# Second weight's operand six built in the first half's chunks from operand seven's sum instead of beside keys and values

## Chip, cores and metric

The kernel runs on one core of one Trainium2 chip. The metric is the device time of one execution in microseconds (us). Three timed runs of the kernel before gave a median of 1102.75 us (1098.13 to 1105.87).

## The reference, cut to what matters

x has 2048 tokens of 576 numbers; the hidden layer of the second block has 4608.

```python
xn = layernorm(x)
q, k, v = split(xn @ wqkv)                  # 32 heads of 18
pq, pk = phi(q), phi(k)                     # phi(t) = (t+1 if t > 0 else exp(t)) + 1e-6
s = (pq @ (pk^T v)) / (pq . sum(pk) + 1e-6) @ wo
h = gelu(xn @ w1 + b1)                      # 2048 x 4608
g = silu(h @ w2 + b2)                       # w2: 4608 x 576
out = x + s * g
```

All of it is in float32. The change concerns how the weight `w2` of the product `h @ w2` is prepared.

## The kernel before

**Number format.** TensorE multiplies in a rounded 32-bit format. Each operand is therefore kept as two tiles: `hi`, the rounded copy, which ScalarE (ACT) makes by a cast, and `lo`, what the rounding left, which VectorE (DVE) makes by subtracting `hi` from the source. A product is then three matmuls per pair of operands: hi times hi, hi times lo, lo times hi.

**Seven products for eight.** Both matrix products of the second block are done as 2x2 block products in a scheme of seven multiplications. For `h @ w2`, `w2` is cut into nine chunks of 512 rows (`NC = 9`, named c), and each chunk into four blocks B00, B01, B10, B11 (row half, then column half), each 128 partitions x 576. The seven right-hand operands are, by their numbers in the code:

```text
1: B00        2: B10        3: B11        7: B11 - B01        5: B01 - B00
6: B11 - (B01 - B00) = operand 7 + B00
4: B10 - operand 7 - B00 = B10 - operand 6
```

The seven left-hand operands come from the gelu results of the same chunk: 1, 2, 4 are gelu tiles themselves, 7, 5, 6, 3 are sums made by GpSimd (POOL) in `HOps.S` (lines 1243 to 1252).

**Stages.** (1) "Keys and values": a loop over 16 tiles of 128 tokens makes the layer norm, keys, values and the state pk^T v (about 0 to 145 us of the span). (2) Queries, attention and the folded output weight, 145 to 283 us. (3) The second block in two halves of 1024 tokens each, nine chunks a half; chunk c of the first half starts at about 283.2 + 44.7 c us. The first half makes the operands of w1 and w2 from the raw weights, multiplies with them and stores them in device memory; the second half loads them back. (4) The end, from about 1065 us.

**Work on w2 in stage 1.** Beside the token tiles, `w2_load` (line 392) loads three blocks of chunk c (864 KB), `w2_sum` (line 402) makes on POOL operand 5 in place of B00 and then operand 6 in place of B11, `w2_hi` (line 407, ACT) and `w2_lo` (line 415, DVE) split each into hi and lo, and `w2_store` (line 420) writes each operand (576 KB) to device memory. `W2_AT` gives the token tile at which chunk c's sums are made; hi, lo and store follow one tile later.

**A chunk of stage 3.** Time in a chunk is counted in 28 steps, each one block of TensorE (PE) work of about 1.6 us. Steps 0 to 6 and 7 to 13 are two "Up" rounds: seven products of w1 operands with x, in the order `UP`, whose PSUM results are combined by DVE and passed through gelu by ACT. Steps 14 to 27 are the seven products with w2 operands in `ORDER`, two PSUM tiles each (q2 = 0, 2); after each, DVE adds the tile into `macc` (line 1292).

```python
UP = (1, 6, 7, 5, 2, 3, 4)
ORDER = (1, 2, 7, 4, 5, 3, 6)
PW2 = {2: 0, 1: 1, 7: 3, 4: 5, 3: 8}                     # operand: step of hi; lo is one step later
for k, i in enumerate(UP):                               # round j of chunk `step`, base = 28 * step
    u.step(i)                                            # seven matmuls, then DVE / ACT on their PSUM
    h.add(j, u.g)
    at_step(base + 7 * j + k)                            # what the plans put at this step
```

The emission order fixes the order of instructions on PE, DVE, ACT and POOL (`in_order`), so a planned instruction that has to wait holds up all that follows on its engine. All DMAs are issued on the queue of SyncE (SP), also in order.

The parts of a chunk that matter here, with "Up 0" and "Up 1" for the two rounds:

- At step 0 POOL makes operand 7 (`sum7`, line 1200), at step 2 operand 4 in two subtractions (`sum4`, line 1205).
- `W2.hi` and `W2.lo` (lines that show in the profile as L812 and L815, the helpers `set_hi` and `set_lo`) make operands 2, 1, 7, 4, 3 at the steps of `PW2`. `W2.lo` also issues the store for the second half, except in chunk 8.
- Operands 5 and 6 are loaded from device memory by `W2.load` (line 1223), for the next chunk at steps 23 and 27 (`W2_SUMS_NEXT`), for chunk 0 at steps 6 and 10 (`W2_SUMS_FIRST`).
- `HOps` (plan `PH`) makes the left-hand operands: `S` on POOL, `hi` on ACT, `lo` on DVE, from step 7 on. A name like (1, 1) is operand 1 of round 1. For operand 1 and 2 of round 0 the lo parts stand at step 10, for (7, 0) at step 11, for (1, 1) at step 12, for (2, 1) at step 13. `S` of (7, 0) stands at step 7, of (5, 0) at step 8, of (6, 0) and (3, 0) at step 11; (6, 0) overwrites the tile that lo of (1, 0) reads.
- The first product (operand 1, step 14) orders its matmuls so that those with the lo part of (1, 1) come last.
- In the second half (chunks 9 to 17) operands come from device memory, and the last chunk works from raw weights.

Of the kernel before, what the change touches and what calls it, by code (L numbers as in the profile page):

```python
# [8 lines left out]
F32 = mybir.dt.float32  # L9
F32R = mybir.dt.float32r  # L10
# [5 lines left out]
P = 128  # L16
S = 2048
D = 576
HD = 288
# [25 lines left out]
def linear_attention_gated_ffn(ctx, tc, x, xT, wqkv, wo, w1, w1e, b1, w2, b2, out):  # L45
    nc = tc.nc
    SUB, MUL, ADD = ALU.subtract, ALU.mult, ALU.add
# [7 lines left out]
    dram = ctx.enter_context(tc.tile_pool(name="dram", bufs=1, space=bass.MemoryType.DRAM))  # L55
# [67 lines left out]
    w1_dram, w2_dram = {}, {}  # L123
# [11 lines left out]
    stw = ph1.enter_context(tc.tile_pool(name="stw", bufs=2, reuse_waits="tile"))  # L135
    w2p = ph1.enter_context(tc.tile_pool(name="w2p", bufs=2, reuse_waits="tile"))
# [249 lines left out]

    T_OPS = (5, 6)
    w2raw, w2op = {}, {}  # L390

    def w2_load(c):
        t = w2p.tile([P, 3, 2, HD], F32, tag="w2r", name=f"w2r{c}")
        nc.sync.dma_start(t.rearrange("p b a d -> p (b a d)"), w2[c][:, D:])
        w2raw[c] = t

    def w2_block(c, i):

        B11, B00, B01 = (w2raw[c][:, k] for k in range(3))
        return {5: (B00, B01, B00), 6: (B11, B11, B00)}[i]  # L400

    def w2_sum(j):
        c, i = j // 2, T_OPS[j % 2]
        dst, a, b = w2_block(c, i)
        nc.gpsimd.tensor_tensor(dst, a, b, op=SUB)

    def w2_hi(j):
        shape = [P, 2, 2, HD]
        if j % 4 < 2:
            w2op[j] = stw.tile(shape, F32R, tag="stw", name=f"w2o{j}")  # L410
        else:
            w2op[j] = w2p.tile(shape, F32R, tag="w2o", name=f"w2o{j}")
        nc.scalar.copy(w2op[j][:, 0], w2_block(j // 2, T_OPS[j % 2])[0])

    def w2_lo(j):
        c, i = j // 2, T_OPS[j % 2]
        t = w2op[j]
        nc.vector.tensor_tensor(t[:, 1], w2_block(c, i)[0], t[:, 0].bitcast(F32), op=SUB)

    def w2_store(j):  # L420
        c, i = j // 2, T_OPS[j % 2]
        w2_dram[c, i] = d = dram.tile([P, 2, 2, HD], F32, name=f"op_{c}_{i}")
        nc.sync.dma_start(d, w2op.pop(j).bitcast(F32))

# [30 lines left out]
    WE_SUMS = {2 * q + 1: q for q in range(WG)}  # L457
    W2_AT = (2, 4, 6, 8, 10, 11, 12, 13, 14)
    W2_LOADS = {0: 0, 1: 1, 3: 2, 5: 3, 7: 4, 9: 5, 11: 6, 12: 7, 13: 8}
    W2_SUMS = {t: (2 * c, 2 * c + 1) for c, t in enumerate(W2_AT)}  # L460

    class XSums:

# [44 lines left out]
        def sum4(self, k):  # L508
            self.tt(self.t, (self.h0, self.l0)[k][:, self.B], self.t, (SUB, ADD)[k])
# [29 lines left out]
    for t in range(NT):  # L539
# [39 lines left out]
        if t + 1 < NTR:  # L579
            if t:  # L580
                k_t, _ = phi(t1, pk, f"k{t}", values)
# [13 lines left out]
            if t == 0:  # L595
                k_t, _ = phi(t1, pk, f"k{t}")
# [591 lines left out]
    class W2:  # L1188
# [10 lines left out]
        def sum7(self):  # L1199
            nc.gpsimd.tensor_tensor(self.src[7], self.src[3], self.src[7], op=SUB)  # L1200

        def sum4(self, k):

            self.src[4] = t = self.src[2]
            nc.gpsimd.tensor_tensor(t, t, self.src[(7, 1)[k]], op=SUB)

        def plain(self, f):
            k = 2 - 2 * (f % 2)
# [16 lines left out]
    class HOps:  # L1225
# [6 lines left out]
        def add(self, pr, g):  # L1232
            for (par, b), t in g.items():
                self.A[pr, b, par] = t
                self.src[{(0, 0): 1, (0, 1): 2, (1, 1): 4, (1, 0): "-"}[b, par], pr] = t
# [236 lines left out]
    )  # L1472


    PW2 = {2: 0, 1: 1, 7: 3, 4: 5, 3: 8}
    W2_SUMS_NEXT = {5: 23, 6: 27}
    W2_SUMS_FIRST = {5: 6, 6: 10}
    W2_NEXT = {1: 15, 2: 17, 7: 19, 4: 21, 5: 23, 3: 25, 6: 27}
    PH = dict(
        S={(7, 0): 7, (5, 0): 8, (6, 0): 11, (3, 0): 11, (7, 1): 13, (5, 1): 14, (6, 1): 15, (3, 1): 15},  # L1480
# [21 lines left out]
    w2t = {}  # L1502
# [8 lines left out]
    for step in range(n_chunks):  # L1511
        half, c = divmod(step, NC)
        base = step * NS
        plain = step == n_chunks - 1
        h = HOps(c)
        if half == 0:
            plan_w1(add, w1t[2 * step + 1], base, **P1)
            add(base, w2t[step].sum7)
            for k in range(2):
                add(base + 2, w2t[step].sum4, k)  # L1520
            for i, at in PW2.items():
                add(base + at, w2t[step].hi, i)
                add(base + at + 1, w2t[step].lo, i)
            if step == 0:
                for i, at in W2_SUMS_FIRST.items():
                    add(at, w2t[0].load, i)
        change = step == NC - 1
        if not plain:
            add(base + (11 if change else 7), load_we, 2 * step + 2)
            add(base + (16 if change else 14), load_we, 2 * step + 3)  # L1530
        if half == 0 and c < NC - 1:
            add(base + 0, make, W1, w1t, 2 * step + 2)
            add(base + 4, make, W1, w1t, 2 * step + 3)
            add(base + 1, lambda n=2 * step + 2, base=base: plan_w1(add, w1t[n], base, **P0))
            make(W2, w2t, step + 1)
            add(base + 22, w2t[step + 1].load_raw)
            for i, at in W2_SUMS_NEXT.items():
                add(base + at, lambda i=i, n=step + 1: w2t[n].load(i))
        elif not plain:
            add(base + (11 if change else 7), make, W1Loaded, w1t, 2 * step + 2)  # L1540
            add(base + (11 if change else 14), load_six, 2 * step + 2)
            add(base + (16 if change else 14), make, W1Loaded, w1t, 2 * step + 3)
            if step + 2 < n_chunks:
                make(W2, w2t, step + 1)
                for i, at in W2_NEXT.items():
                    add(base + at + 10 * change, lambda i=i, n=step + 1: w2t[n].load(i))
            else:
                make(W2, w2t, step + 1)

                w = w2t[step + 1]  # L1550
                add(base + 7, w.load_raw)
                for f in range(CF):
                    add(base + 22 + f, lambda f=f, w=w: (w.plain(f), w.hi(("p", f))))
                    add(base + 24 + f, w.lo, ("p", f))
        if not plain:
            if half == 0 and c == NC - 1:
                for k, at in X_AT.items():
                    add(base + at, load_x_part, k)
                add(base + 14, lambda: x_new.update(rs=load_rests(0)))
                add(base + 25, silu_first, C11)  # L1560
                for k in range(2):
                    add(base + 26 + k, combine, C12, nc.vector, slice(2 * k, 2 * k + 2))
                    add(base + 26 + k, combine, C21, nc.gpsimd, slice(2 * k, 2 * k + 2))
            for what in ("S", "hi", "lo"):
                for (i, pr), at in PH[what].items():
                    add(base + at, getattr(h, what), i, pr)
        if half == 1 and c == 0:
            add(base, silu_first, C12)
            add(base, silu_first, C21)
            add(base, combine, C22, nc.vector, slice(0, 2))  # L1570
            add(base + 1, combine, C22, nc.vector, slice(2, 4))
            add(base + 1, silu_first, C22)
        if half == 1 and c:
            for k in range(2):
                tiles = {}
                def load(k=k, t=7 + c, tiles=tiles):
                    tiles[0] = finish_tiles(k)
                    finish_load(t, k, tiles[0])
                add(base, load)
                add(base + 4, lambda k=k, t=7 + c, tiles=tiles: finish(t, k, tiles[0]))  # L1580
        if plain:
            for m in (C12, C21, C22):
                add(base + 4, combine, m, nc.gpsimd)
            for t, at in enumerate((6, 7, 12, 13, 5, 12, 12, 12)):
                add(base + at, load_xs, t)
            for b, f, at, lo in (
                (0, 0, 7, 8), (0, 1, 8, 9), (1, 0, 10, 10), (1, 1, 10, 11), (0, 2, 11, 12),
                (0, 3, 12, 13), (1, 3, 13, 13), (1, 2, 13, 13),
            ):
                add(base + at, tail_split, b, f)  # L1590
                add(base + lo, tail_lo, b, f)
        for j in range(CF // 2):
            n = 2 * step + j
            u = Up(n, w1t.pop(n), xs)
            for k, i in enumerate(UP):
                u.step(i)
                h.add(j, u.g)
                at_step(base + 7 * j + k)
        if plain:
            break  # L1600
        held = {}
        for k, i in enumerate(ORDER):
            for q2 in (0, 2):
                product(c, i, q2, [h.ops[i, 0], h.ops[i, 1]], w2t[step].ops[i], held)
                at_step(base + 14 + 2 * k + q2 // 2)
        if half == 0 and c == NC - 1:
            xs = x_operands(*(x_new[k] for k in ("h0", "l0", "h1", "l1", "s1", "s2", "s4", "rs")))
# [50 lines left out]
```

## Time and profile before

| what | us |
|---|---|
| median of three timed runs (lowest, highest) | 1102.75 (1098.13, 1105.87) |
| span of the profiled execution, first to last instruction | 1096.2 |
| stage 1 (keys and values), about | 0 to 145 |
| stage 2 (queries, attention), about | 145 to 283 |
| first half of the second block, nine chunks of 44.7 us | 283 to 686 |
| second half, eight chunks of 44.7 us and the plain last one | 686 to 1096 |

The profiled execution has no time listed beside its span; the span is 1.9 us under the fastest timed run and 6.6 us under the median. The mean granted clock of TensorE was 0.999.

How to read the rows: a row of the timeline has start and duration in us, engine, line, operation, output<-inputs by the program's names, shape, and in brackets the idle time of the engine ahead of it with what ended it. PEld is the loading of the stationary operand into TensorE, which runs ahead of the matmuls. A row of the stretches ("windows") has the busy time and the count of each engine, then the granted clock, the share of the DMA engines that was busy, and GB/s. Consecutive instructions of one engine overlap by some 0.08 us in these rows. The names `w__4896` and `w__4937` are chunk 3's operands 4 and 3.

### The profile page before, as it was taken

The numbers are of one execution on the slowest core, as the hardware profiler recorded it, in microseconds if no ns is written. First come the engines' busy times: TensorE is split into PE (matmuls) and PEld (weight loads), VectorE is DVE, ScalarE is ACT, GpSimd is POOL, SyncE is SP. The second block draws the span as 40 slices with busy tenths as digits, with TensorE's granted clock in tenths as the row PEclk, the third lists the DMA queues.
The fourth block names the chain that finished last, engine by engine and source line by source line (L and its number), as shares of the span: only waits on it lengthen the run. The fifth ranks groups of instructions, "written<-read, shape, count | busy, mean of one in ns | idle before, by whom it ended". The sixth has DMA issues, their size and how long they took to land.

```text
span 1096.2 us, 18083 instructions
## 1 busy us (share of the span) xinstructions
PE 1088.2 (99%) x6702; PEld 1008.8 (92%) x6702; DVE 829.5 (76%) x1132; ACT 491.3 (45%) x844; POOL 471.5 (43%) x403
## 2 busy tenths in 40 slices
PE   9999999999999999999999999999999999999998
PEld 8999989999898998989989989899898998989987
DVE  7787748888798888888888888667475584764856
ACT  6555555555545455454453544524234243242442
POOL 3676434323546446464554553424234143242340
PEclk9999999999999999999999999999999999999999
DMA  7898834675959558486585769978676676767452
GB/s 248 264 274 274 309 137 149 206 248 186 333 221 350 182 220 322 160 320 224 189 332 175 284 237 400 391 248 289 215 241 219 210 231 212 238 219 224 126 184 87
DMA packets 88400, 262.54 MB, mean 239 GB/s; under 512 B 11894, under 2 KB 24182, under 8 KB 85624
## 3 DMA queue, kind: packets, MB, share of 16 engines
q1 hardware_dynamic: 88312, 261.38, 69.3%
q8 instruction: 53, 0.87, 0.3%
q14 instruction: 35, 0.29, 0.1%
HBM read 164.24 MB, written 95.17 MB: 237 GB/s over the span
## 4 chain that ended last, share of the span: by engine, by line
PE 99%; DVE 1%; ACT 0%; issue 0%; POOL 0%; DVEq 0%; POOLq 0%
PE pm L1286 35%; PE a L1147 10%; PE e L1147 10%; PE zy L1147 10%; PE pk L321 6%; PE pq L321 5%; PE ps_s L788 5%; PE b L1147 5%; PE pv L321 4%; PE pd L1402 2%; PE ps_kva L382 1%; PE ptp L770 1%; PE ps_kw L707 1%; PE warm L369 0%; DVE wkv_l L364 0%; PE ps_kvb L382 0%
## 5 line engine op out<-in xcount | busy, mean ns | idle before, releaser
L1292 DVE TENSOR_TENSOR macc<-pm,macc 128x576 f32<-128x576 f32 x218 | 163.9, 752 | 49.9 <-PE pm L1286 48.4
L812 ACT CAST h_h<-g 128x512 fp32r<-128x512 f32 x204 | 121.9, 621 | 132.7 <-PE pm L1286 131.5
L815 DVE TENSOR_TENSOR h_l<-g,h_h 128x512 fp32r<-128x512 f32 x204 | 161.8, 800 | 0.0
L1252 POOL TENSOR_TENSOR mid<-g 128x512 f32<-128x512 f32 x34 | 43.9, 1292 | 108.1 <-ACT g L1155 108.1
L1246 POOL TENSOR_TENSOR g<-g 128x512 f32<-128x512 f32 x34 | 54.9, 1616 | 49.5 <-DVE h_l L815 28.4
L1155 ACT ACTIVATE g<-b,b1c 128x512 f32<-128x512 f32 x36 | 24.8, 690 | 102.5 <-DVE b L1173 102.5
L1164 ACT COPY mid<-a 128x512 f32<-128x512 f32 x36 | 21.1, 585 | 95.3 <-PE a L1147 95.3
L858 POOL TENSOR_TENSOR w1raw<-w1raw 128x256 f32<-128x256 f32 x18 | 13.3, 737 | 116.8 <-ACT h_h L812 68.2
L1167 DVE TENSOR_TENSOR mid<-b,mid 128x512 f32<-128x512 f32 x36 | 24.8, 690 | 45.0 <-PE b L1147 41.8
L1374 POOL TENSOR_TENSOR fin1l<-fin1h,fin1l 128x288 f32<-128x288 f32 x8 | 6.5, 811 | 118.4 <-DMA fin1l<-s_dram 69.6
L1249 POOL TENSOR_TENSOR g<-g 128x512 f32<-128x512 f32 x34 | 55.2, 1623 | 2.7
L1147 PE MATMUL a<-h0r,wa 128*128 128x512 f32 x144 | 50.4, 390 | 0.0
L1147 PE MATMUL a<-xh,wa 128*128 128x512 f32 x144 | 50.4, 390 | 0.0
L815 DVE TENSOR_TENSOR h_l<-mid,h_h 128x512 fp32r<-128x512 f32 x34 | 48.8, 1436 | 1.2
L1155 ACT ACTIVATE g<-e,b1c 128x512 f32<-128x512 f32 x36 | 24.8, 690 | 51.9 <-DVE e L1180 51.9
L753 POOL TENSOR_TENSOR pbuf<-phiq,den 128x576 f32<-128x576 f32 x16 | 19.4, 1213 | 63.6 <-DVE den L752 63.6
L1243 POOL TENSOR_TENSOR g<-g 128x512 f32<-128x512 f32 x34 | 44.1, 1296 | 2.7
L1180 DVE TENSOR_TENSOR e<-e,mid 128x512 f32<-128x512 f32 x36 | 24.8, 690 | 22.3 <-PE e L1147 22.3
L1170 DVE TENSOR_TENSOR mid<-zy,mid 128x512 f32<-128x512 f32 x36 | 24.9, 691 | 19.8 <-PE zy L1147 19.8
L1173 DVE TENSOR_TENSOR b<-e,mid 128x512 f32<-128x512 f32 x36 | 25.2, 700 | 18.5 <-PE e L1147 17.4
L321 PE MATMUL pk<-wkv_h,xh 128*128 128x288 f32 (+1 forms) x160 | 38.2, 321 | 0.4 <-ACT xh L248 0.4
L321 PE MATMUL pk<-wkv_l,xh 128*128 128x288 f32 (+1 forms) x160 | 38.4, 321 | 0.0
(857 smaller groups left out, 3646.5 us busy)
## 6 DMA issues: line engine op xcount, KB each, us to landing
we<-we_dram SPq DMA_DIRECT2D x36, 448.0 KB
w2raw<-w SPq DMA_DIRECT2D x10, 1152.0 KB
op<-w2o SPq DMA_DIRECT2D x18, 576.0 KB
w1raw<-w SPq DMA_DIRECT2D x18, 512.0 KB
op_a<-wa SPq DMA_DIRECT2D x18, 512.0 KB
op_c<-wc SPq DMA_DIRECT2D x18, 512.0 KB
op_d<-wd SPq DMA_DIRECT2D x18, 512.0 KB
wc<-op_c SPq DMA_DIRECT2D x18, 512.0 KB
```

Of the source, the lines that this page charges most:

```text
L321: nc.tensor.matmul(ps[:, h, : ws.stop - ws.start], st, w[:, k, ws], start=(begin and i == 0), stop=(end and i == len(seq) - 1), skip_group ...
L788: nc.tensor.matmul(ps[:, h, :HD], st[:, k, :], w[:, k, h * HD : (h + 1) * HD], start=(i == 0), stop=(i == len(seq) - 1),)
L812: nc.scalar.copy(pair[0], src)
L815: eng.tensor_tensor(pair[1], src, pair[0].bitcast(F32), op=SUB)
L1147: nc.tensor.matmul(ps, st, mv, start=first and n == 0, stop=n == len(seq) - 1, skip_group_check=True,)
L1155: nc.scalar.activation(g, ps, AF.Gelu_apprx_tanh, bias=b1c[:, f : f + 1])
L1243: tt(src[5, pr], A(1, 0), A(1, 1), op=ADD)
L1246: tt(src[6, pr], src[5, pr], A(0, 0), op=SUB)
L1249: tt(src[3, pr], A(0, 1), src[6, pr], op=SUB)
L1252: tt(src[7, pr], A(0, 0), A(1, 0), op=SUB)
L1286: nc.tensor.matmul(ps[:, q, :HD], hs[p][st][:, cs], m[:, p, :], start=(n == 0 and i not in CHAIN), stop=(n == 5), skip_group_check=True,)
L1292: nc.vector.tensor_tensor(dst, src, dst, op=ADD)
```

## The change

Stage 1 no longer loads B11 and no longer makes operand 6: per chunk it loads two blocks (576 KB), makes one sum, one hi, one lo and one store. In the first half's chunks POOL makes operand 6 as operand 7 plus B00 (in place of B00, so after B00's own hi and lo), and operand 4 as B10 minus operand 6, both now at step 3; ACT and DVE then make hi and lo of operand 6 too, and it is stored for the second half except in chunk 8. Operand 4's hi and lo move from steps 5 and 6 to 6 and 7, operand 6's are at 7 and 8, operand 3's move from 8 and 9 to 9 and 10. The loads of operand 6 in the first half are gone. The second half's loads are as before.

```diff
-    T_OPS = (5, 6)
     def w2_load(c):
-        t = w2p.tile([P, 3, 2, HD], F32, tag="w2r", name=f"w2r{c}")
-        nc.sync.dma_start(t.rearrange("p b a d -> p (b a d)"), w2[c][:, D:])
+        t = w2p.tile([P, 2, 2, HD], F32, tag="w2r", name=f"w2r{c}")
+        nc.sync.dma_start(t.rearrange("p b a d -> p (b a d)"), w2[c][:, 2 * D :])
-    def w2_block(c, i):
-        B11, B00, B01 = (w2raw[c][:, k] for k in range(3))
-        return {5: (B00, B01, B00), 6: (B11, B11, B00)}[i]
-    def w2_sum(j):
-        c, i = j // 2, T_OPS[j % 2]
-        dst, a, b = w2_block(c, i)
-        nc.gpsimd.tensor_tensor(dst, a, b, op=SUB)
-    def w2_hi(j):
-        shape = [P, 2, 2, HD]
-        if j % 4 < 2:
-            w2op[j] = stw.tile(shape, F32R, tag="stw", name=f"w2o{j}")
-        else:
-            w2op[j] = w2p.tile(shape, F32R, tag="w2o", name=f"w2o{j}")
-        nc.scalar.copy(w2op[j][:, 0], w2_block(j // 2, T_OPS[j % 2])[0])
+    def w2_sum(c):
+        B00, B01 = (w2raw[c][:, k] for k in range(2))
+        nc.gpsimd.tensor_tensor(B00, B01, B00, op=SUB)
+    def w2_hi(c):
+        w2op[c] = w2p.tile([P, 2, 2, HD], F32R, tag="w2o", name=f"w2o{c}")
+        nc.scalar.copy(w2op[c][:, 0], w2raw[c][:, 0])
...
-    W2_SUMS = {t: (2 * c, 2 * c + 1) for c, t in enumerate(W2_AT)}
+    W2_SUMS = {t: (c,) for c, t in enumerate(W2_AT)}
...
-        def sum4(self, k):
+        def sum6(self):
+            self.src[6] = t = self.src[1]
+            nc.gpsimd.tensor_tensor(t, self.src[7], t, op=ADD)
+        def sum4(self):
             self.src[4] = t = self.src[2]
-            nc.gpsimd.tensor_tensor(t, t, self.src[(7, 1)[k]], op=SUB)
+            nc.gpsimd.tensor_tensor(t, t, self.src[6], op=SUB)
...
-    PW2 = {2: 0, 1: 1, 7: 3, 4: 5, 3: 8}
-    W2_SUMS_NEXT = {5: 23, 6: 27}
-    W2_SUMS_FIRST = {5: 6, 6: 10}
+    PW2 = {2: 0, 1: 1, 7: 3, 4: 6, 6: 7, 3: 9}
...
             add(base, w2t[step].sum7)
-            for k in range(2):
-                add(base + 2, w2t[step].sum4, k)
+            add(base + 3, w2t[step].sum6)
+            add(base + 3, w2t[step].sum4)
             for i, at in PW2.items():
                 add(base + at, w2t[step].hi, i)
                 add(base + at + 1, w2t[step].lo, i)
             if step == 0:
-                for i, at in W2_SUMS_FIRST.items():
-                    add(at, w2t[0].load, i)
+                add(6, w2t[0].load, 5)
...
             add(base + 22, w2t[step + 1].load_raw)
-            for i, at in W2_SUMS_NEXT.items():
-                add(base + at, lambda i=i, n=step + 1: w2t[n].load(i))
+            add(base + 23, w2t[step + 1].load, 5)
```

More of the change, by code (lines that the diff above doesn't have):

```diff
@@ L385, in state, with w2_lo, w2_store @@
             )
-    T_OPS = (5, 6)
     w2raw, w2op = {}, {}
     def w2_load(c):
-        t = w2p.tile([P, 3, 2, HD], F32, tag="w2r", name=f"w2r{c}")
-        nc.sync.dma_start(t.rearrange("p b a d -> p (b a d)"), w2[c][:, D:])
+        t = w2p.tile([P, 2, 2, HD], F32, tag="w2r", name=f"w2r{c}")
+        nc.sync.dma_start(t.rearrange("p b a d -> p (b a d)"), w2[c][:, 2 * D :])
         w2raw[c] = t
-    def w2_block(c, i):
-        B11, B00, B01 = (w2raw[c][:, k] for k in range(3))
-        return {5: (B00, B01, B00), 6: (B11, B11, B00)}[i]
-    def w2_sum(j):
-        c, i = j // 2, T_OPS[j % 2]
-        dst, a, b = w2_block(c, i)
-        nc.gpsimd.tensor_tensor(dst, a, b, op=SUB)
-    def w2_hi(j):
-        shape = [P, 2, 2, HD]
-        if j % 4 < 2:
-            w2op[j] = stw.tile(shape, F32R, tag="stw", name=f"w2o{j}")
-        else:
-            w2op[j] = w2p.tile(shape, F32R, tag="w2o", name=f"w2o{j}")
[L413 to L423, printed above, removed]
+    def w2_sum(c):
[4 more added lines that the diff above has]
+        nc.scalar.copy(w2op[c][:, 0], w2raw[c][:, 0])
+    def w2_lo(c):
+        t = w2op[c]
+        nc.vector.tensor_tensor(t[:, 1], w2raw[c][:, 0], t[:, 0].bitcast(F32), op=SUB)
+    def w2_store(c):
+        w2_dram[c, 5] = d = dram.tile([P, 2, 2, HD], F32, name=f"op_{c}_5")
+        nc.sync.dma_start(d, w2op.pop(c).bitcast(F32))
     we = {}
```

## The prediction

> **What bounds the kernel now.** I read the page's totals first (busy time and share of the span), then the windows by stage (busy time and count of PE, PEld, DVE, ACT and POOL, clock, DMA share, GB/s), then one chunk of the first half engine by engine.
>
> ```profile
> span 1096.2 us, 18083 instructions
> PE 1088.2 (99%) x6702; PEld 1008.8 (92%) x6702; DVE 829.5 (76%) x1132; ACT 491.3 (45%) x844; POOL 471.5 (43%) x403
> ```
>
> ```profile
> 41.02:142.41 101.39, 101.39 (x626) 98.48 (x625) 80.96 (x99) 56.51 (x111) 68.00 (x62) 1.00 0.89 280
> 417.32:462.04 44.72, 44.72 (x267) 40.81 (x267) 39.18 (x52) 21.28 (x37) 23.43 (x19) 1.00 0.67 246
> ```
>
> ```profile
> 417.32:439.58 22.26, 22.26 (x100) 18.40 (x100) 18.89 (x25) 12.39 (x22) 12.96 (x10) 1.00 0.97 363
> ```
>
> TensorE is busy in all of stage 1's steady part (101.39 of 101.39 us) and in all of chunk 3 (44.72 of 44.72). Only 8.0 us of the span are without a matmul. So work taken from another engine can give back next to nothing; work put on another engine costs nothing until TensorE has to wait for it. The engine to watch is DVE: 39.18 of 44.72 us in a chunk, 18.89 of 22.26 in its two Up rounds, where the change adds its work.
>
> **What the change takes away.** In stage 1, half of these:
>
> ```profile
> L405 POOL TENSOR_TENSOR w2r<-w2r 128x576 f32<-128x576 f32 x18 | 28.8, 1598 | 15.6 <-DVE phik L340 8.5 <-DMA w2r<-w 6.4
> ...
> L418 DVE TENSOR_TENSOR w2o<-w2r,w2o 128x576 fp32r<-128x576 f32 x18 | 19.1, 1098 | 0.2
> ...
> L413 ACT CAST w2o<-w2r 128x576 fp32r<-128x576 f32 x18 | 11.5, 672 | 2.5 <-POOL w2r L405 2.5
> ```
>
> That is 14.4 us of POOL, 9.6 of DVE, 5.8 of ACT, nine stores of 576 KB, and nine loads shorter by 288 KB. TensorE's full row covers all of it: 0 us. The bounds: no loss, and a gain of no more than the 8.0 us that TensorE is idle anywhere, most of it at the start and the end, where none of this work stands; I take 0.
>
> In the first half nine loads of operand 6 go and eight stores of the same size come. DMA engines are 97% busy in the Up rounds; the load left at the head of that stretch and the store comes at its foot, so its bytes stay as they are.
>
> ```profile
> 434.78 0.33 SPq L809 DMA_DIRECT2D op<-w__4937  x1
> ...
> 462.84 0.38 SPq L1223 DMA_DIRECT2D w__5265<-op  x1
> ```
>
> On SP's queue the new store stands just ahead of the first row and the load of the second row goes. What queues behind the later stores of operands 4 and 6 is the load of `we` for the next chunk, delayed by 1 to 2 us with over 20 us in hand: 0 us. POOL has one sum and one subtraction in place of two subtractions of the same shape, behind the same instructions: 0 us.
>
> **What it adds, on the path.** Per chunk one cast on ACT and one DVE subtraction, and operand 4's pair moves one step back. The price depends on where TensorE next waits for DVE. These are chunk 3's rows of the timeline from the end of Up 0 on: DVE, then ACT, then POOL, then TensorE.
>
> ```profile
> 429.97 0.69 DVE L1184 TENSOR_TENSOR zy<-zy,mid 128x512 f32<-128x512 f32 x1
> 430.78 0.76 DVE L815 TENSOR_TENSOR w__4896<-w2raw,w__4896 128x576 fp32r<-128x576 f32 x1
> 431.89 0.69 DVE L1167 TENSOR_TENSOR mid<-b,mid 128x512 f32<-128x512 f32 x1 [0.36 <-ACT mid L1164]
> 433.27 0.69 DVE L1170 TENSOR_TENSOR mid<-zy,mid 128x512 f32<-128x512 f32 x1 [0.69 <-PE zy L1147]
> 433.88 0.87 DVE L815 TENSOR_TENSOR w__4937<-w2raw,w__4937 128x576 fp32r<-128x576 f32 x1
> 434.86 0.70 DVE L1173 TENSOR_TENSOR b<-e,mid 128x512 f32<-128x512 f32 x1
> 435.47 1.28 DVE L815 TENSOR_TENSOR h_l<-g,h_h 128x512 fp32r<-128x512 f32 x2
> 436.83 1.63 DVE L815 TENSOR_TENSOR h_l<-mid,h_h 128x512 fp32r<-128x512 f32 x1
> 438.38 0.69 DVE L1180 TENSOR_TENSOR e<-e,mid 128x512 f32<-128x512 f32 x1
> 438.98 1.18 DVE L815 TENSOR_TENSOR h_l<-g,h_h 128x512 fp32r<-128x512 f32 x1
> ...
> 442.80 0.76 DVE L1292 TENSOR_TENSOR macc<-pm,macc 128x576 f32<-128x576 f32 x1 [0.78 <-PE pm L1286]
> ```
>
> ```profile
> 430.08 0.66 ACT L812 CAST w__4896<-w2raw 128x576 fp32r<-128x576 f32 x1
> 430.69 0.69 ACT L1155 ACTIVATE g<-zy,b1c 128x512 f32<-128x512 f32 x1
> 431.28 0.58 ACT L1164 COPY mid<-a 128x512 f32<-128x512 f32 x1
> ```
>
> ```profile
> 431.46 1.30 POOL L1252 TENSOR_TENSOR mid<-g 128x512 f32<-128x512 f32 x1 [3.23 <-ACT g L1155]
> 432.84 1.30 POOL L1243 TENSOR_TENSOR g<-g 128x512 f32<-128x512 f32 x1
> 436.32 1.58 POOL L1246 TENSOR_TENSOR g<-g 128x512 f32<-128x512 f32 x1 [2.19 <-ACT g L1155]
> 437.99 1.62 POOL L1249 TENSOR_TENSOR g<-g 128x512 f32<-128x512 f32 x1
> ```
>
> ```profile
> 436.25 1.52 PE L1147 MATMUL e<-s,wc 128*128 128x512 f32 x6
> ...
> 440.61 0.32 PEld L1286 LDWEIGHTS pm<-w__4829,h_l 128*128 128x128 f32 x2
> ```
>
> The row at 438.98 is the lo part of (1, 1); it ends at 440.16. The row at 440.61 is the first load that needs it. The slack is 0.45 us. From 434.86 to there DVE has no idle time, so whatever DVE has more to do behind 434.86 comes straight off it. The change puts operand 3's lo (now at step 10) exactly there.
>
> The POOL rows show a second price. The lo part at 436.83 takes 1.63 us where the pair ahead of it takes 0.64 each: POOL's sum of 436.32 runs until 437.90, and it ends 0.56 behind that. The lo part at 438.98 ends 0.55 behind POOL's 439.61. POOL's own sum at 437.99, caught behind DVE's end at 438.46, ends 1.15 after it. DVE rows that take one input from PSUM (0.69, 0.70) show no such thing. So: a DVE subtraction caught behind a POOL sum ends 0.55 after it (0.62 for 576 columns), a POOL sum caught behind DVE 1.15 after it.
>
> The walk, each start 0.08 before the end of the row ahead, cross-engine starts 0.03 after the end waited for:
>
> - ACT: gelu 430.69 as before; hi of 4 now behind it, 431.28 to 431.94; copy of `mid` 431.89 to 432.47; hi of 6 to 433.04.
> - DVE: lo of 4 starts at 431.97 instead of 430.78, now caught behind POOL's sum (ends 432.76): ends 433.38. POOL's next sum ends 434.53.
> - `mid<-b` 433.30 to 433.99. Lo of 6, caught behind POOL's 434.53, ends 435.15. `mid<-zy` ends 435.76, `b<-e` 436.38 (before: 435.56). TensorE's matmul of 436.25 adds into the bank that `b<-e` reads: it waits 0.15.
> - Lo of 3 ends 437.06, lo of (1, 0) 437.66, lo of (2, 0) 438.26. POOL's sum, which overwrites what (1, 0) reads, is released at 437.7, caught behind (2, 0), ends 439.41.
> - Lo of (7, 0) ends 439.97, POOL's next sum 441.12, `e<-e` 440.58, lo of (1, 1) 441.67.
> - The load at 440.61 starts at 441.70: TensorE stands 1.09 us, the 0.15 included.
>
> Later in the chunk DVE had 0.78 us idle waiting for TensorE (row 442.80), and `macc` keeps its place ahead of the chained product, so the lag ends there and does not add up from chunk to chunk. Ends far apart: if nothing collides, DVE is late by one lo (0.68 beyond overlap) less 0.45 of slack, 0.26 with the 0.03: 2.3 us in all. If each caught instruction took its full solo time behind the other (0.68 or 0.76, and 1.30), the same walk ends the lo of (1, 1) at 442.65 and TensorE stands 2.07: 18.6 us. I take 1.09, since the caught rows of this very place gave its two constants.
>
> The Trainium skill, page "SBUF — State Buffer", section "Who interferes with whom", says that a DVE instruction with two SBUF inputs contends with a GpSimd instruction that reads SBUF, and that the one issued first holds the shared pair for the whole instruction while the other fully blocks. The rows agree that one waits for the other, though the one caught ends 0.55 after, not a full 0.68, so here it had done a little beforehand. By the rule taken strictly the sum would be the 18.6 us just given.
>
> All nine chunks of the first half carry the same rows; the first and the last:
>
> ```profile
> 304.83 1.18 DVE L815 TENSOR_TENSOR h_l<-g,h_h 128x512 fp32r<-128x512 f32 x1
> ...
> 662.57 1.18 DVE L815 TENSOR_TENSOR h_l<-g,h_h 128x512 fp32r<-128x512 f32 x1
> ```
>
> ```profile
> 306.46 0.32 PEld L1286 LDWEIGHTS pm<-w__3385,h_l 128*128 128x128 f32 x2
> ...
> 664.20 0.32 PEld L1286 LDWEIGHTS pm<-w__7225,h_l 128*128 128x128 f32 x2
> ```
>
> The slack is 0.45 in both. So 9 x 1.09 = 9.8 us: a span of 1106.0. The median of the runs lies 6.55 above the span; added to it, 1112.55, say 1112.5, slower by 0.9%. One per cent (11.0 us) is about what a measurement of this kernel can tell from no change.
>
> **The rivals.**
>
> - *No collision.* DVE and POOL slide past each other, only the shift of one lo remains: +2.3 us, 1105. For it: DVE is idle 0.36 and 0.69 in this very place. Against: the POOL sums follow gelu and DVE, they slide along. Chance 0.16.
> - *Full blocking.* Caught instructions take their full time: +18.6 us, 1121; anything from 1.22 us a chunk on passes one per cent. For it: the lo part of 1.63 us. Against: 0.55, twice. Chance with all that lies between 1.22 and 2.07: 0.34.
> - *Not slower: stage 1 gives it back.* Timed runs lie 1.9 to 9.7 us above the span. If that excess is the transfers of stage 1 (89% busy), 8.0 MB less at 280 GB/s is 28 us of transfer time, which could bring a run down to the span: -6.5 us, 1096. It decides only if TensorE waits for transfers there and nothing stands in the chunks. Against: its full row. Chance 0.06, half of it by over one per cent with what I don't see.
> - *The change doesn't do what it says.* Operand 6 made late for its product (step 26)? It is there at step 8, 18 steps early; nothing speaks for it, and it gets no chance of its own.
>
> **How the numbers follow.** The forecast (0.8 to 1.2 us a chunk) has 0.44. Slower by over 1%: 0.34 of full blocking and what lies between, and 0.03 of the forecast's upper edge with the scatter of runs: 0.37. Faster by over 1%: 0.03. Within 1%: 0.60. The range reaches from 1102 (no collision, less run scatter) to 1119 (1.8 us a chunk), which leaves out the last of full blocking and the gain; the forecast's own range is 1109 to 1114.
>
> **What would show it.** Right: TensorE's loads in the first product wait for DVE once a chunk, chunks of 45.5 to 46 us in the first half and still 44.7 in the second; lo of operand 4 over 1.2 us long; stage 1 as long as before with DVE 9 us less busy. Wrong: a first-half chunk under 45.0 us (no collision), over 46.2 (full blocking), a wait at another place, or a shorter stage 1.

## The result, and the profile after

The changed kernel takes 1111.83 us (median of four runs, 1111.43 to 1112.2). The kernel before takes 1100.82 us, the median of the three runs above and one more beside the changed kernel (1098.13 to 1105.87). That is a ratio of 1.009, 95% interval 1.0061 to 1.012, 11.0 us slower. The forecast was 1112.5. The near hit of the time hides two errors. The span was forecast at 1106.0 and came out at 1110.4, 14.2 us longer than before instead of 9.8. The median was forecast 6.55 above the span and lies 1.4 above it. That 4.4 too little and 5.1 too much nearly cancel is luck, and most of what follows is about these two errors.

The page's first lines and the windows of the kernel after (busy time and count of PE, PEld, DVE, ACT, POOL, then clock, DMA share, GB/s): stage 1, chunk 3 of the first half, one chunk of the second half.

```profile
span 1110.4 us, 18032 instructions
PE 1094.7 (99%) x6702; PEld 1008.3 (91%) x6702; DVE 826.0 (74%) x1132; ACT 491.7 (44%) x844; POOL 459.8 (41%) x394
```

```profile
41.02:142.14 101.12, 101.12 (x625) 98.24 (x624) 63.61 (x90) 51.19 (x101) 52.97 (x54) 1.00 0.81 215
421.98:468.36 46.38, 45.48 (x267) 40.76 (x267) 40.77 (x53) 21.90 (x38) 23.82 (x19) 1.00 0.67 237
...
722.49:767.17 44.68, 44.68 (x268) 40.80 (x268) 28.34 (x39) 14.56 (x25) 14.86 (x13) 1.00 0.74 250
```

Stage 1 ends 0.27 us earlier and DVE is 17 us less busy in it. A chunk of the first half takes 46.37 us instead of 44.72, 1.65 more; nine of them are 14.9. A chunk of the second half is as before. Now PE is not busy all of the chunk (45.48 of 46.38). The 0.90 us of idle time are only part of the 1.65: the matmuls behind a wait take longer too (the six behind the first wait 1.67 us for 1.52). What its weight loads waited for (engine, tile, line, what it waited for: us in total, times, longest):

```profile
PEld pm L1276 <- DVE h_l L802: 6.2, 9, 0.7
PEld e L1134 <- DVE b L1160: 5.6, 9, 0.6
PEld pm L1276 <- ACT h_h L799: 4.3, 9, 0.5
```

Three waits, each once in each of the nine chunks. The kernel before had none of them. Chunk 3 again, DVE first; these rows stand 4.66 us later than those of before, as chunk 3 itself does (421.98 for 417.32). `w__4859`, `w__4876` and `w__4904` are operands 4, 6 and 3.

```profile
436.63 1.39 DVE L802 TENSOR_TENSOR w__4859<-w2raw,w__4859 128x576 fp32r<-128x576 f32 x1 [1.32 <-ACT w__4859 L799]
437.95 0.68 DVE L1154 TENSOR_TENSOR mid<-b,mid 128x512 f32<-128x512 f32 x1
438.55 1.25 DVE L802 TENSOR_TENSOR w__4876<-w2raw,w__4876 128x576 fp32r<-128x576 f32 x1
439.73 0.68 DVE L1157 TENSOR_TENSOR mid<-zy,mid 128x512 f32<-128x512 f32 x1
440.51 0.70 DVE L1160 TENSOR_TENSOR b<-e,mid 128x512 f32<-128x512 f32 x1
441.12 0.75 DVE L802 TENSOR_TENSOR w__4904<-w2raw,w__4904 128x576 fp32r<-128x576 f32 x1
441.78 1.29 DVE L802 TENSOR_TENSOR h_l<-g,h_h 128x512 fp32r<-128x512 f32 x2
442.99 1.79 DVE L802 TENSOR_TENSOR h_l<-mid,h_h 128x512 fp32r<-128x512 f32 x1
444.70 0.69 DVE L1167 TENSOR_TENSOR e<-e,mid 128x512 f32<-128x512 f32 x1
445.30 1.18 DVE L802 TENSOR_TENSOR h_l<-g,h_h 128x512 fp32r<-128x512 f32 x1
...
454.43 0.74 DVE L1282 TENSOR_TENSOR macc<-pm,macc 128x576 f32<-128x576 f32 x1
```

POOL, then the loading side of TensorE, in the same chunk:

```profile
436.12 1.29 POOL L1242 TENSOR_TENSOR mid<-g 128x512 f32<-128x512 f32 x1 [3.23 <-ACT g L1142]
437.49 1.70 POOL L1233 TENSOR_TENSOR g<-g 128x512 f32<-128x512 f32 x1
```

```profile
441.26 1.24 PEld L1134 LDWEIGHTS e<-s,wc 128*128 128x128 f32 x6 [0.62 <-DVE b L1160]
...
446.53 0.30 PEld L1276 LDWEIGHTS pm<-w__4782,h_l 128*128 128x128 f32 x2 [0.67 <-DVE h_l L802]
```

```profile
454.37 0.32 PEld L1276 LDWEIGHTS pm<-w__4815,h_h 128*128 128x128 f32 x2
...
455.30 0.30 PEld L1276 LDWEIGHTS pm<-w__4859,h_h 128*128 128x128 f32 x2 [0.47 <-ACT h_h L799]
```

The lo part of operand 4 (436.63) is caught behind POOL's sum of 436.12, takes 1.39 for 0.76, and ends 0.61 after it. POOL's next sum is caught behind that in turn and ends 1.17 after it; the lo part of operand 6 is caught behind this sum and ends 0.61 after it. `b<-e` comes at 440.51 and the load of 441.26 waits for it: first wait. Operand 3's lo follows, then the lo parts of the first product, and (1, 1) ends at 446.48: second wait. The third stands at the first load of operand 4's product, 455.30. The view names ACT's cast, but the tile that this product adds into is freed by the DVE row of 454.43, which ends at 455.17; which of the two it is was tried below.

### The profile page after: what moved, and what is told of

Same layout as the page of the kernel before. It is cut to its first block, busy times and chain, and to the rows that moved or that the text cites. A ratio compares the mean times of both kernels' runs of the same rounds, so it can differ in the third digit from the quotient of the medians.

```text
span 1110.4 us, 18032 instructions
## 1 busy us (share of the span) xinstructions
PE 1094.7 (99%) x6702; PEld 1008.3 (91%) x6702; DVE 826.0 (74%) x1132; ACT 491.7 (44%) x844; POOL 459.8 (41%) x394
## 4 chain that ended last, share of the span: by engine, by line
PE 87%; DVE 7%; issue 2%; DMA 2%; POOL 1%; ACT 1%; SPq 0%; DVEq 0%; POOLq 0%
PE pm L1276 30%; PE a L1134 8%; PE zy L1134 8%; PE e L1134 7%; PE pk L321 6%; PE pq L321 5%; PE ps_s L775 5%; PE b L1134 5%; PE pv L321 4%; DVE h_l L802 4%; PE pd L1392 2%; PE ps_kva L382 1%; PE ptp L757 1%; PE ps_kw L694 1%; DVE macc L1282 1%
## 5 line engine op out<-in xcount | busy, mean ns | idle before, releaser
L1236 POOL TENSOR_TENSOR g<-g 128x512 f32<-128x512 f32 x34 | 54.9, 1614 | 60.9 <-DVE h_l L802 59.5
L1239 POOL TENSOR_TENSOR g<-g 128x512 f32<-128x512 f32 x34 | 55.2, 1624 | 2.7
L1233 POOL TENSOR_TENSOR g<-g 128x512 f32<-128x512 f32 x34 | 47.6, 1401 | 2.7
L775 PE MATMUL ps_s<-kw_h,th 128*128 128x288 f32 x160 | 35.5, 303 | 0.0
```

The costliest lines, as they stand in the source:

```text
L775: nc.tensor.matmul(ps[:, h, :HD], st[:, k, :], w[:, k, h * HD : (h + 1) * HD], start=(i == 0), stop=(i == len(seq) - 1),)
L1233: tt(src[5, pr], A(1, 0), A(1, 1), op=ADD)
L1236: tt(src[6, pr], src[5, pr], A(0, 0), op=SUB)
L1239: tt(src[3, pr], A(0, 1), src[6, pr], op=SUB)
```

## The experiments

**Theories.** Two errors need a cause. For the chunks, A: the cost is place, not load. DVE is late where the new and moved lo parts stand ahead of something TensorE waits for, and is made later by being caught behind POOL sums; put elsewhere, the same work is free. B, the rival: the first half's chunks have no room left on DVE and ACT, so the work costs about the same wherever it stands. For the second error, C: stage 1's lighter transfers bring timed runs down to the span. D: they are worth nothing, and the spread of the runs of before (8 us here) comes from elsewhere. Each experiment has runs of the kernel before beside it. For operand 6 later, operand 4's pair back, the third wait and stage 1 alone these are the same 30 runs, median 1099.68 (1097.25 to 1107.8). For order without work, before again, transfers kept and work kept they are another 26, median 1100.88 (1098.47 to 1108.59).

**Operand 6 later, 4 and 3 where they were.** On the changed kernel:

```diff
-    PW2 = {2: 0, 1: 1, 7: 3, 4: 6, 6: 7, 3: 9}
+    PW2 = {2: 0, 1: 1, 7: 3, 4: 5, 3: 8, 6: 19}
```

> The changed kernel with operands 4 and 3 back at their old steps (hi 5 and 8, lo 6 and 9) and operand 6's hi and lo at steps 19 and 20, where no POOL sum runs and DVE has idle time. Theory A (TensorE waits because of the place of these lo parts: ahead of b<-e, of lo (1, 1) and of operand 7's macc, caught behind POOL sums): all waits go, chunks of 44.7 us in the first half, span about 1096, time 1097 to 1099. Theory B (the price is the load that DVE and ACT take on, wherever it stands): chunks stay near 46.3 us, time 1109 to 1112.

Measured: 1097.17 us (1096.73 to 1097.61, 12 runs), ratio to before 0.9973 (0.9961 to 0.9985). In its chain of waits (start, length) the products of chunks 2 and 3 start 44.72 us apart:

```profile
394.95 22.46 PE pm L1276 x168
439.67 22.46 PE pm L1276 x168
```

All of the added work is there, and all of the cost is gone: A, against B. This version also beats the kernel before. Its gain over it is that of stage 1, below: the chunks cost what they did.

**Only operand 4's pair back.**

```diff
-    PW2 = {2: 0, 1: 1, 7: 3, 4: 6, 6: 7, 3: 9}
+    PW2 = {2: 0, 1: 1, 7: 3, 4: 5, 6: 7, 3: 9}
```

> The changed kernel with only operand 4's hi and lo back at steps 5 and 6; operand 6 stays at 7 and 8, operand 3 at 9 and 10. Theory A, by the walk of the rows: lo of 4 is no longer caught behind the POOL sum, b<-e is on time again, lo (1, 1) is still late by 0.26 us and operand 7's macc by 0.1: chunks of 45.0 to 45.1, span about 1099, time about 1100.5. Theory B: chunks of 46.3, time 1111.

Measured: 1103.18 us (1102.97 to 1103.75), ratio 1.003 (1.0011 to 1.0048), span 1101.5, chunks of 45.39. Its loads waited for:

```profile
PEld pm L1276 <- ACT h_h L799: 4.3, 9, 0.5
...
PEld pm L1276 <- DVE h_l L802: 1.9, 9, 0.2
```

```profile
315.28 13.03 PE pm L1276 x96
360.68 13.03 PE pm L1276 x96
```

The first wait is gone and the second falls from 0.67 to 0.21 (0.26 by the walk). The lo part of operand 4 stands ahead of POOL's sum again and takes 0.76 us, as in the kernel before:

```profile
432.54 0.76 DVE L802 TENSOR_TENSOR w__4849<-w2raw,w__4849 128x576 fp32r<-128x576 f32 x1
```

So operand 4's pair, one step later, made 0.98 of the 1.65 us a chunk. But the third wait stayed whole, where I had expected 0.1: a miss of the expectation by 0.35 a chunk.

**What the third wait is for.** On the changed kernel, one lo part moved behind one macc on DVE:

```diff
-            (4, 1): 17, (5, 1): 18, (5, 0): 19,
+            (4, 1): 18, (5, 1): 18, (5, 0): 19,
```

> The changed kernel with the lo part of left operand (4, 1) one step later (18 for 17), behind operand 7's first macc on DVE; ACT's casts stay as they are. If TensorE's third wait of a chunk (0.4 us, at the first matmul of operand 4's product) is for that macc, which frees the PSUM tile: it goes, chunks of 46.0 us, 3.6 us in all, time about 1108. If it waits for ACT's cast, as the row names it: chunks stay 46.37, time 1111.8.

Measured: 1107.27 us (1106.95 to 1107.66), 4.6 under the changed kernel, span 1105.5. The chain of waits has the products of chunks 0 and 1 45.86 apart, and of the three rows of waits two are left:

```profile
307.31 21.32 PE pm L1276 x158
353.17 21.32 PE pm L1276 x158
```

```profile
PEld pm L1276 <- DVE h_l L802: 6.3, 9, 0.7
PEld e L1134 <- DVE b L1160: 5.5, 9, 0.6
```

ACT's casts were not touched and the wait went, so it was for DVE's macc; the row that named ACT named the event that ended last by 0.03 us (455.20 for the cast, 455.17 for the macc). The kernel before says the same: its two casts at this place were still running when operand 4's product started at 449.01.

```profile
448.67 1.14 ACT L812 CAST h_h<-g 128x512 fp32r<-128x512 f32 x2 [2.06 <-PE pm L1286]
```

The chunk is 0.14 shorter than the 46.0 expected, because the edit also ends a wait of some 0.08 that the kernel before had here (see the third wait below).

**Both of these edits together.** On the changed kernel:

```diff
-    PW2 = {2: 0, 1: 1, 7: 3, 4: 6, 6: 7, 3: 9}
+    PW2 = {2: 0, 1: 1, 7: 3, 4: 5, 6: 7, 3: 9}
...
-            (4, 1): 17, (5, 1): 18, (5, 0): 19,
+            (4, 1): 18, (5, 1): 18, (5, 0): 19,
```

> The changed kernel with both edits that each took one wait away: operand 4's hi and lo at steps 5 and 6, and the lo part of (4, 1) at step 18. Theory A: the waits are separate and add up; of the three only the wait for lo (1, 1) is left, 0.2 us a chunk: chunks of 44.95 us, time 1099. If the macc's wait is only passed on to another place (DVE is simply late), chunks stay at 45.4 and the time at 1103.

Measured: 1098.28 us (1098.11 to 1098.66), ratio 0.9974 (0.9958 to 0.9991) to runs of before with a median of 1101.12, chunks of 44.88; one wait of the three is left, 0.2 us:

```profile
304.80 22.62 PE pm L1276 x168
349.69 22.62 PE pm L1276 x168
```

The waits are separate and add up.

**Order without work.** On the kernel before, nothing added:

```diff
-    PW2 = {2: 0, 1: 1, 7: 3, 4: 5, 3: 8}
+    PW2 = {2: 0, 1: 1, 7: 3, 4: 6, 3: 9}
```

> The kernel before with nothing added, only operand 4's hi and lo one step later (6, 7) and operand 3's (9, 10); operand 6 is still made in stage 1. Theory A (order and lock): lo of 3 stands ahead of the lo parts of the first product and shifts lo (1, 1) past its load by 0.2 to 0.3 us and operand 7's macc by 0.45, as with operand 4 moved back: chunks of 45.4 us, span 1102, time 1103 to 1106. Theory B (load): no work is added, chunks stay 44.7, time as before.

Measured: 1109.16 us (1106.76 to 1110.2, 4 runs), ratio 1.0069 (1.0047 to 1.0091). The chunks are 45.40 us as expected, so 6.1 us are order alone; the lo part of operand 4 takes 1.39 us here too, with no work added.

```profile
311.45 9.33 PE pm L1286 x68
356.86 9.33 PE pm L1286 x68
```

The time is 3 us above the expected range. The profiled execution is the longest of the four (1110.2), and in it the excess is not in the chunks but in stage 1. Waits, then the chain of waits around the place:

```profile
ACT xh L293 <- DMA we_dram<-w1h: 9.1, 1, 9.1
```

```profile
PE pk L321 <- ACT xh L293: 4.8, 1, 4.8
```

```profile
83.67 13.99 DMA bc<-st_dram
97.83 1.56 POOL xt L282
...
103.31 2.07 DVE w1h L450
105.39 9.44 DMA we_dram<-w1h
114.93 0.73 ACT xh L293
115.71 6.29 PE pk L321 x28
```

A 128 KB load took 14.0 us to land; it made a POOL sum late, that the last staging of w1, that its store; the store took 9.4 us, and until it had landed ACT could not write the next x tile in its place. TensorE stood 4.8 us. The other three runs were not profiled.

**Where the spread of before lies.** First the kernel before once more, unedited; then three kernels that settle C against D.

> The kernel before as it is, to see where its spread of some 8 us lies. If the extra time is inside the span (TensorE waiting somewhere), each run's span follows its time at a fixed distance of 1.7 us; if it lies outside, the spans stay near 1096.

Measured: 1098.83 us (1097.27 to 1107.38). The spans follow the times: 1095.6 for 1097.27, 1098.0 for 1099.74, 1102.8 for 1104.54, 1105.7 for 1107.38. The extra time is inside the span, and the distance of 1.7 is fixed.

Stage 1's part of the change alone, on the kernel before (`w2_load` to `w2_store` as in the changed kernel):

```diff
-            nc.sync.dma_start(t.bitcast(F32), w2_dram[self.n % NC, i])
+            nc.sync.dma_start(t.bitcast(F32), w2_dram[self.n % NC, 5 if i == 6 else i])
```

> The kernel before with stage 1's part of the change alone: operand 6 is left out, nothing makes it, and wherever it was loaded the stored operand 5 is loaded instead; loads and all work in the chunks are as before. Theory C (stage 1's lighter transfers bring the timed runs down to the span): span about 1096, timed runs close together at 1097 to 1098.5. Theory D (stage 1's relief is worth nothing, and the spread of the timed runs of before has another cause): median within 1 us of the runs of before beside it, with the same spread of some 8 us.

Measured: 1097.1 us (1096.86 to 1099.93, 12 runs, all but one under 1097.7), ratio 0.9974 (0.996 to 0.9989).

The same with the transfers of before:

```diff
-        t = w2p.tile([P, 2, 2, HD], F32, tag="w2r", name=f"w2r{c}")
+        t = w2p.tile([P, 3, 2, HD], F32, tag="w2r", name=f"w2r{c}")
...
+        for i in (5, 6):
+            w2_dram[c, i] = d = dram.tile([P, 2, 2, HD], F32, name=f"op_{c}_{i}")
+            nc.sync.dma_start(d, t)
```

> The kernel before without the sum, hi and lo of operand 6 in stage 1, but with its transfers: three blocks are loaded and operand 5's tile is stored a second time in operand 6's place (which is so left out of the result). If the transfers of stage 1 make the spread of before, it stays: median 1099 to 1101, runs up to 1103 and more. If the work on POOL, DVE and ACT makes it, the runs lie close together at 1097 to 1098.

Measured: 1099.44 us (1097.74 to 1105.35), ratio 0.9991 (0.9974 to 1.0009).

The kernel before with its work, without these transfers:

```diff
-        B11, B00, B01 = (w2raw[c][:, k] for k in range(3))
-        return {5: (B00, B01, B00), 6: (B11, B11, B00)}[i]
+        B00, B01 = (w2raw[c][:, k] for k in range(2))
+        return {5: (B00, B01, B00), 6: (B01, B01, B00)}[i]
...
+        if i == 5:
+            w2_dram[c, i] = d = dram.tile([P, 2, 2, HD], F32, name=f"op_{c}_{i}")
+            nc.sync.dma_start(d, t)
```

> The kernel before with the sum, hi and lo of a sixth operand in stage 1 (from the two blocks that are loaded, so not the right one), but without its store and without the third block's load; the loads in the chunks take operand 5 in its place. If transfers make the spread: runs close together at 1097 to 1098. If work makes it: median 1099 to 1101 with runs up to 1103 and more.

Measured: 1097.09 us (1096.86 to 1097.47), ratio 0.9952 (0.9931 to 0.9973). Stage 1's windows, of the kernel that kept the transfers, then of the one that kept the work:

```profile
41.02:142.20 101.18, 100.02 (x613) 96.71 (x613) 59.05 (x90) 50.64 (x99) 49.93 (x48) 1.00 0.96 279
```

```profile
41.02:142.20 101.18, 101.18 (x625) 98.28 (x624) 79.15 (x99) 56.02 (x110) 70.94 (x63) 1.00 0.75 215
```

With the work out and the transfers kept (DMA engines 96% busy) the spread stays; with the work kept and the transfers out (75%) it is gone. In the first row TensorE is not full either: 100.02 of 101.18. What is missing is the wait found in the run with the order alone, at the same place and behind the same store. The kernel before, profiled again, has it too. First the kernel with the transfers kept, then before again:

```profile
PE pk L321 <- ACT xh L293: 1.2, 1, 1.2
PE pk L321 <- ACT xh L293: 1.0, 1, 1.0
```

ACT waited 8.2 and 8.0 us for the store there, against 9.1 in the run with the order alone and 3.5 in the first profile of before. None of the seven profiles with the lighter transfers has TensorE wait there; with the full transfers three of four have it. So C: it is the 8 MB of transfers, not the work, that some runs pay for, and the changed kernel has this gain: its own runs lie 0.8 us apart.

## Why the prediction was right, and where it was wrong

- **The time: right by luck.** The sum for the chunks was 9.8 us and 14.9 came; the distance of the median from the span was 6.55 and 1.4 came. By the prediction's own signs the chunk of 46.37 is outside 45.5 to 46 and over the 46.2 that was to mean full blocking. It was not full blocking, as the last point shows, but a third wait that the sum had at nothing: with it ended, the chunk is 45.86.
- **Bound and covers: right.** Stage 1's work on three engines was worth nothing by itself: with the work kept and the transfers out the time is 1097.09, with both out 1097.1. DVE was freed of 17 us where I had 9.6, half of its row. The rest is in rows that stayed and got shorter, such as the staging of w1 (from 9.1 to 5.5 us). The second half is unchanged.
- **Mechanism of the first two waits: right.** TensorE waits once a chunk for lo (1, 1), because lo of 3 stands ahead of it and lo of 4 and 6 are caught behind POOL. The two constants held: 0.61 measured for 0.62, 1.17 for 1.15. The walk has (1, 1) ending at 441.67, which is 446.33 on the later chunk; it ended at 446.48.
- **First wait: mis-sized.** I priced the wait of `e` for `b<-e` at 0.15, counted from the matmul of 436.25. What waits is the load ahead of it, which should have started 0.22 after the load at 440.46; it stood 0.58, and `b<-e` itself came 0.17 later than walked. Only the 0.17 enters the sum: DVE has no idle time from `b<-e` to the lo part of (1, 1), so that part comes when it does however long TensorE stood before. The load that needs it is 1.26 late for my 1.09.
- **Third wait: the step that failed.** "`macc` keeps its place ahead of the chained product, so the lag ends there" was looked up for the product after the first only. Operand 4's product adds into operand 7's tile, and there the kernel before had nothing in hand:

```profile
448.12 0.74 DVE L1292 TENSOR_TENSOR macc<-pm,macc 128x576 f32<-128x576 f32 x1
...
449.01 0.51 PE L1286 MATMUL pm<-w__4896,h_h 128*128 128x288 f32 x2
```

  The macc ends at 448.86 and the pair of matmuls starts at 449.01, taking 0.51 where such a pair takes 0.43: it was waiting by some 0.08 already. What is left of the 1.65 for this wait is 0.39 a chunk, 3.5 us. The edit that ended it took off 0.51, since it ended those 0.08 as well. The sum in the chunks is 1.65, not 1.09: 14.9 us, not 9.8.
- **Stage 1 at nothing: wrong, and it hid the other errors.** The rival "stage 1 gives it back" had a chance of 0.06, on the strength of one full row of TensorE. That row is of an execution without the delay. The runs' distance from the span (1.9 to 9.7 us) was the evidence, and it was of this cause: each run lies 1.7 above its own span, the rest is delay in stage 1. In the 30 runs of before the median lies 2.4 us above the fastest. It did not decide the sign, but it took some 3 us off: 14.2 more in span against 11.0 in the median.
- **Full blocking: wrong in its time.** The Trainium skill, page "SBUF — State Buffer", section "SBUF: two separate sides", has one of the two wait for the other's whole instruction; in kind the trace agrees. By it taken strictly the caught lo parts would end 0.76 after POOL; they ended 0.61 after, and the 18.6 us of that case did not come.

What stays open: why single transfers of stage 1 land late in some runs and not in others. The experiments show that taking bytes away ends it, not which transfer starts it. The delay stands at one place in three profiles, but only one of them is of a long run; where the other long runs lose their time was not seen.

## What to carry to other kernels

Where one engine is busy throughout, price an edit by the slack at each point where that engine waits for the edited one, and look at all such points down the chunk: the tightest was not the nearest. A wait's row names the event that ended last; where two end within 0.03 us, move one of them and see. If timed runs lie further above the profiled span than a run lies above its own (1.7 us here), the profile has not shown what they pay for.

## What the runs showed of the hardware

After TensorE had stood 4.8 us in stage 1 (kernel with the order alone), its clock came back at half speed. Three windows of that execution, from the end of the wait on:

```profile
115.70:118.10 2.40, 2.39 (x9) 2.34 (x10) 2.34 (x3) 2.39 (x5) 1.71 (x1) 0.54 0.04 15
118.10:119.30 1.20, 1.20 (x6) 1.17 (x5) 1.20 (x2) 1.18 (x3) 0.00 (x0) 0.50 0.00 0
119.30:120.50 1.20, 1.20 (x9) 1.20 (x8) 1.20 (x3) 0.08 (x1) 0.00 (x0) 1.00 0.75 303
```

The clock column reads 0.54, 0.50, then 1.00: some 3.6 us at half speed, so that 28 matmuls took 6.29 us for 4.47, and the wait of 4.8 cost 1.8 more. The chunks' waits of 0.2 to 0.7 us left the clock at 1.00, and so did the waits of 1.0 and 1.2 us in stage 1. In the 26 runs of before beside this kernel, all 13 above 1101 us have a mean granted clock of 0.994 to 0.997 and the other 13 one of 0.998 to 1.000, as they would if TensorE stood that long there too. The Trainium skill, page "TensorE: Matmul & The Clock Gate", section "Part 1: The HAM clock gate (the "warmup" mystery)", says that an idle stretch of about 3.4 us drops the clock to half and that as long a busy one restores it; this execution agrees on both counts.
